# PSUM banks of stage one, and one sigmoid for the output gates, in a gated mix of memory attention and SwiGLU

## The chip, the cores and the metric

The kernel runs on one core of one Trainium2 chip. A core has TensorE (PE, with its weight loads listed apart as PEld), VectorE (DVE), ScalarE (ACT), GpSimd (POOL) and SyncE (SP, which here only issues DMAs), an on-chip memory for tiles, and the matmul accumulator PSUM, which this program uses as eight tiles, `bank0` to `bank7`. Engines run their own instruction lists in order and wait for each other by semaphores. The metric is the device time of one execution in microseconds; lower is better. Times are from one profiled execution unless a median of runs is named.

## The reference

`x` is 2048 tokens of width 576. Its output is `g * a + (1 - g) * b` with a gate per token, a memory attention `a` and a feed-forward `b`:

```python
g = sigmoid((x * gate_w).sum(-1, keepdims=True))
a = A(x, wq, wk, wv, wo, beta)          # 32 heads of 18, 4 segments of 512 tokens
b = (silu(x @ w_gate) * (x @ w_up)) @ w_down      # hidden width 4608
out = g * a + (1 - g) * b
```

For each of the four segments the attention computes, per head,

```python
p = softmax(qs @ ks.T * scale + mask)         # causal inside the segment
a_dot = p @ vs
pq = phi(qs)                                  # phi(t) = t + 1 if t > 0 else exp(t)
a_mem = (pq @ M) / (pq @ z + 1e-6)            # what earlier segments left
o = sigmoid(beta) * a_mem + (1 - sigmoid(beta)) * a_dot
M = M + phi(ks).T @ vs; z = z + phi(ks).sum(0)
```

and ends with `o @ wo`.

## The kernel before

**Precision.** Most products are formed from a high and a low part of each operand: `split` copies the high part on ACT (line 129) and subtracts on DVE for the low part (line 130), and three products of parts are accumulated.

**Stage one** goes over the four segments `s`. Each segment has two halves.

The first half is a loop over nine q/k *chains* (`qk`). A chain is 14 matmuls of 512 columns into one bank (`products`, line 152), then ACT copies (line 356), relu and exp (361, 362), DVE subtractions (363), and, where `phi` is wanted, a last DVE read of the bank (369). In segment 0 the chains take their banks in turn from banks 0 to 4 (`first_tile`; a trio starts together on banks 0, 1 and 2), in later segments from 0, 1 and 2 (`chain_tile`). From segment 1 on `upd_gen` is interleaved: it transposes `phi(k)` of the segment before into banks 5, 6 and 7, copies it to `kt` (line 420), multiplies it with the values (line 411) into banks 3 and 4 (`pair_tile`), and at the end adds the masked result to the memory (DVE line 434, POOL line 435).

The second half is a loop of eight steps `n`. Each has a value step and, from segment 1 on, a memory step. `v_step` is 14 matmuls of 288 or 290 columns (line 152) into a bank from `v_tile`, in turn 5, 6 and 7; then ACT reads the bank (385, 386), DVE subtracts (387), in segment 0 DVE copies (389), ACT takes the second part (392) and POOL the third (393). The column `x @ gate_w` comes out with the values and is copied into `gl` (391). `mem_step` is six matmuls (line 457) into a bank from `mem_tile`, in turn 3, 4 and 2 and carried on from segment to segment; DVE divides and scales (460 to 464). After the last value step of each segment the sigmoid of the gates of that segment is formed: one ACT exponential (398) and three DVE operations (399 to 401) on 4 columns, into `gg` and `g1`.

In segment 3 the first weights of the feed-forward are prepared between the value steps. `w_make` gives a list of small operations, each with a place in time: sums on POOL (257), high parts on ACT (`HIGH`, line 261), low parts on DVE (`LOW`, line 264), stores of what is kept (267). Those with a place under 8 are dealt out, two or three a step; the rest go to stage two's queue.

**Stage two** has 72 units, two halves of the tokens times 36 tiles of the hidden width. A unit is seven products (`seven`, lines 996 and 999), on which ACT and DVE build the gated activation (`a` in bank 0, `xx` in bank 1, `y` in bank 2; line 1053 copies bank 0 to bank 1 after the first product, and the third product adds to bank 0). After each product `tick` runs one *beat*: functions that `defer` placed there, some groups of the down projection (line 856), and a step of the attention generator `att_gen` (scores line 725, row minimum 731, exponential 743, causal select 751, casts 757 and 758, a DMA transpose of the probabilities `p` into `pt` 762, values 773 and 774). The loads of a unit are deferred in the same way. When attention is through, `c_open` defers the loads and splits of `wo`. ACT swaps its table for Silu in every unit and back for exp (lines 1070 and 989).

**The end** transposes the attention rows, multiplies with `wo` and mixes with `gg` and `g1`.

The order on each engine is the order in which the Python code issues the operations; nothing reorders them. The release of a bank to its next user is a semaphore wait on the last reader.

Of the kernel before, what the change touches and what calls it, by code (L numbers as in the profile page):

```python
# [12 lines left out]
F32 = mybir.dt.float32  # L13
# [3 lines left out]
AF = mybir.ActivationFunctionType  # L17
OP = mybir.AluOpType
AX = mybir.AxisListType

P = 128
# [10 lines left out]
E = DH + 1  # L32
# [14 lines left out]
LOW = (5, 6, 7, 8, 9, 10, 11)  # L47
# [13 lines left out]
def f32(ap):  # L61
    return ap.bitcast(F32)
# [3 lines left out]
def gated_mix(ctx, tc, xT, xrest, wf, wfr, wfh, wd, wv, wo, beta, cmask, ident, bmask, out):  # L66
    nc = tc.nc
    ctx.enter_context(tc.manual_schedule())

    def pool(st, name, bufs, side="left", space=None):  # L70
        if space is None:
            return st.enter_context(tc.tile_pool(name=name, bufs=bufs, side=side))
        return st.enter_context(tc.tile_pool(name=name, bufs=bufs, space=space))
# [12 lines left out]
    ps = pool(ctx, "ps", 1, space=bass.MemoryType.PSUM)  # L86
# [4 lines left out]
    gg = consts.tile([P, 16], F32, name="gg")  # L91
    g1 = consts.tile([P, 16], F32, name="g1")
# [6 lines left out]
    def banks(*ids):  # L99
        turn = cycle(ids)  # L100
        return lambda shape=(P, L): ps.tile(list(shape), F32, name=f"bank{next(turn)}")
# [2 lines left out]
    half_tile = banks(5, 6)  # L104
    pair_tile = banks(3, 4)
    first_tile = banks(0, 1, 2, 3, 4)
    mem_tile = banks(3, 4, 2)
    lone_tile = banks(7)
    v_tile = banks(5, 6, 7)
    a_tile = banks(0)  # L110
    x_tile = banks(1)
    y_tile = banks(2)
# [112 lines left out]
    def op_tile():  # L225
        return wop.tile([P, 2, 2, P], F32R, name="wo_")
# [19 lines left out]
    def r_fetch(f):  # L246
        nc.sync.dma_start(f32(rhs[f % 2][:96]).rearrange("p j n -> p (j n)"), rc[f // 4, :, f % 4])

    def w_make(half, f):
        g, u = wraw_of.pop(f)  # L250
        ops = wops[half, f] = [None] * 7
        a11, a12, a21, a22 = g[:, 0:2], g[:, 2:4], u[:, 0:2], u[:, 2:4]
        src = [a11, None, None, a12, None, None, a22]

        def total(j, p, q, sub=True):
            src[j] = rp.tile([P, 2, P], F32, name="ws", bufs=3)
            (nc.gpsimd.tensor_sub if sub else nc.gpsimd.tensor_add)(src[j], p(), q())  # L257

        def high(j):
            ops[j] = op_tile()  # L260
            nc.scalar.activation(ops[j][:, 0], src[j], AF.Copy)

        def low(j):
            nc.vector.tensor_sub(ops[j][:, 1], src[j], f32(ops[j][:, 0]))

        def keep(j):
            nc.sync.dma_start(wc[f, j], f32(ops[j]).rearrange("p a k n -> p (a k n)"))

        todo = [(LEAD - 2, lambda: total(1, lambda: a21, lambda: a22, False)),
                (LEAD - 1, lambda: total(2, lambda: src[1], lambda: a11)),  # L270
                (LEAD + 2, lambda: total(4, lambda: a11, lambda: a21)),
                (LEAD + 4, lambda: total(5, lambda: a12, lambda: src[2]))]
        for j in range(7):
            todo += [(HIGH[j], lambda j=j: high(j)), (LOW[j], lambda j=j: low(j))]
            if half == 0 and f < KEPT:
                todo.append((LEAD + j + 3, lambda j=j: keep(j)))
        return sorted(todo, key=lambda t: t[0])
# [3 lines left out]
    with ExitStack() as st:  # L281
# [11 lines left out]
        gl = vp.tile([P, 16], F32, name="gl")  # L293
# [82 lines left out]
        def v_step(s, hf, i):  # L376
            n = 288 + 2 * hf
            t = v_tile()
            products(t[:, :n], [z[:, P * i:P * i + P] for z in x_side(*xs_of[s])], w_mov(vw[hf], n))
            pv = t[:, :288].rearrange("p (h e) -> p h e", e=DH)  # L380
            fv = vf[:, i, 16 * hf:16 * hf + 16, 0:DH]
            v = vps[hf]
            r1 = sp.tile([P, 16, DH], F32, name="r1")
            if s:
                nc.scalar.activation(fv, pv, AF.Copy)
            nc.scalar.activation(v[:, i, :, 0, 0:DH], pv, AF.Copy)
            nc.vector.tensor_sub(r1, pv, v[:, i, :, 0, 0:DH])
            if not s:
                nc.vector.tensor_copy(fv, pv)
            if hf:  # L390
                nc.vector.tensor_copy(gl[:, 4 * s + i:4 * s + i + 1], t[:, 288:289])
            nc.scalar.activation(v[:, i, :, 1, 0:DH], r1, AF.Copy)
            nc.gpsimd.tensor_sub(v[:, i, :, 2, 0:DH], r1, v[:, i, :, 1, 0:DH])
            if i == 3:
                late.append((vd[s, hf], v))
                if hf:
                    z = slice(4 * s, 4 * s + 4)
                    nc.scalar.activation(gg[:, z], gl[:, z], AF.Exp, scale=-1.0)
                    nc.vector.tensor_scalar_add(gg[:, z], gg[:, z], 1.0)
                    nc.vector.reciprocal(gg[:, z], gg[:, z])  # L400
                    nc.vector.tensor_scalar(g1[:, z], gg[:, z], -1.0, 1.0, op0=OP.mult, op1=OP.add)

        def upd_gen(s):
            acc = [pair_tile([P, 3, MW]), pair_tile([P, 2, MW])]
# [41 lines left out]
        def mem_step(s, i, bank):  # L446
            c = slice(P * i, P * i + P)
            if bank == 0:
                oms[s, i] = sp.tile([P, D], F32, name="om") if s < 3 else sp.tile([P, D], F32, name="q3", bufs=4)
            om = oms[s, i]  # L450
            dn = sp.tile([P, 16], F32, name="dn")
            M = Mm[s % 2]
            t = mem_tile([P, 16, E])
            todo = [z for z in MT if z[0] == bank]
            for n, (_, k, lo_, hi_) in enumerate(todo):
                a = HR[k][0]
                nc.tensor.matmul(t[:, lo_ - 16 * bank:hi_ - 16 * bank, :], phi[s, k, 0][:, c],  # L457
                                 M[:, k, (lo_ - a) * E:(hi_ - a) * E],
                                 start=(n == 0), stop=(n == len(todo) - 1), skip_group_check=True)
            nc.vector.tensor_scalar_add(dn, t[:, :, DH], 1e-6)  # L460
            nc.vector.reciprocal(dn, dn)
            nc.vector.tensor_mul(dn, dn, bg[:, 16 * bank:16 * bank + 16])
            ov = om[:, 288 * bank:288 * bank + 288].rearrange("p (h e) -> p h e", e=DH)
            nc.vector.tensor_mul(ov, t[:, :, 0:DH], dn[:, :, None].to_broadcast([P, 16, DH]))
            if bank:
                late.append((med[4 * s + i], oms.pop((s, i))))
# [129 lines left out]
        for s in range(NSEG):  # L596
# [41 lines left out]
            if s == 3:  # L638
                qst_.close()
                rp = pool(ctx, "rp", 4, side="right")  # L640
                wop = pool(ctx, "wop", 7, side="right")
                kq = pool(ast, "kq", 1, side="right")
                for i in range(NST):
                    qst.append(kq.tile([P, 2, L], BF, name=f"qst{i}"))
                    kst.append(kq.tile([P, 2, L], BF, name=f"kst{i}"))
                for i in range(2):
                    mbs.append(kq.tile([P, 8], F32, name=f"mb{i}"))
                for z in range(2):
                    for j, b, kt in ((0, 2, z), (3, 2, 2 + z), (5, 3, 2 + z)):
                        XO[j][z] = xs_of[b][0][kt]  # L650
                wraw_of[0] = [w_load(0, u) for u in range(2)]
                for z in range(2):
                    rhs.append(wop.tile([P, 7, P], F32R, name=f"rh{z}", bufs=1))
                start = w_make(0, 0)
            for n in range(8):
                hf, i = divmod(n, 4)
                flush()
# [31 lines left out]
    with ExitStack() as st:  # L689
# [3 lines left out]
        def defer(k, fn):  # L693
            while len(due) < k:
                due.append([])
            due[k - 1].append(fn)
# [172 lines left out]
        def c_open():  # L869
            if cps:  # L870
                return
            ast.close()
            cps.append(pool(st, "cp", 2, side="right"))
            for hf in range(2):
                wos.append(cps[0].tile([P, 2, NT, 288], F32R, name=f"wo{hf}", bufs=1))
            for n, (hf, z) in zip((1, 2, 4, 5, 8, 9), ((0, 0), (0, 1), (0, 2), (1, 0), (1, 1), (1, 2))):
                wo_load(n, hf, slice(96 * z, 96 * z + 96))
            defer(2, lambda: tiles.update({0: c_load(0)}))
            defer(6, lambda: tiles.update({1: c_load(1)}))

        def wo_load(n, hf, c):
            box = []
# [9 lines left out]
        def c_load(n):  # L892
            tt = order[n]
            o = cps[0].tile([P, 640], F32, name="o", bufs=3)
            nc.sync.dma_start(o[:, 0:D], atd[tt])
            me = None
            if tt >= 4:
                me = cps[0].tile([P, D], F32, name="me", bufs=3)
                nc.sync.dma_start(me, med[tt])
            return o, me  # L900
# [210 lines left out]
        for n in range(17):  # L1111
# [6 lines left out]
            if n:  # L1118
                tt = order[n - 1]
                ff = ffs.pop(n - 1)  # L1120
                for hf in range(2):
                    c = slice(288 * hf, 288 * hf + 288)
                    t = chain_tile()
                    products(t[:, :288], ops, w_mov(wos[hf], 288))
                    downs(1)
                    if hf == 0:
                        nc.vector.tensor_scalar_mul(ff, ff, g1[:, tt:tt + 1])
                    nc.vector.scalar_tensor_tensor(ff[:, c], t[:, :288], gg[:, tt:tt + 1], ff[:, c],
                                                   op0=OP.mult, op1=OP.add)
# [61 lines left out]
```

## Time and profile before

| | us |
|---|---|
| median of 3 runs (1752.46 to 1756.5) | 1755.48 |
| the profiled execution | 1755.81 |
| its span, first to last instruction | 1754.1 |
| PE busy | 1718.9 |
| DVE busy | 1373.2 |
| ACT busy | 1094.7 |
| POOL busy | 935.5 |
| mean granted TensorE clock | 0.995 |

Stage one fills the first 228 us of the span, stage two goes to about 1664, and the end takes the rest. A timeline row gives the start, the duration, engine, line, operation, tile written and tiles read, and the number of instructions merged; in brackets stand the idle time of the engine before it and the instruction that ended it. A duration holds the instruction's own pipeline, so consecutive rows of one engine overlap a little; start to start is the better measure. In a row of the chain of waits stand start, length, engine, tile and line, and how many instructions were merged.

### The profile page before, as it was taken

What the parts mean: (1) busy time and instruction counts of PE and PEld (TensorE: products, weight loads), DVE (VectorE), ACT (ScalarE), POOL (GpSimd) and SP (SyncE); (2) the same over time, 40 slices, a digit from 0 to 9 for tenths busy, and PEclk for the clock granted to TensorE, in tenths of its full rate; (3) what the DMA queues carried; (4) which work ended last, traced back from release to release, by engine and by line L of the source; (5) the groups of instructions that cost most, each with busy time, mean ns of one, the idle gap of its engine ahead of it and who ended that gap; (6) DMA issues with size and microseconds to landing.
All of it is one profiled execution on the core that took longest, in us unless ns stands there. A gap on an engine that the chain in (4) does not pass through costs nothing.

```text
span 1754.1 us, 34945 instructions
## 1 busy us (share of the span) xinstructions
PE 1718.9 (98%) x11868; PEld 1487.7 (85%) x11868; DVE 1373.2 (78%) x3239; ACT 1094.7 (62%) x2201; POOL 935.5 (53%) x1194
## 2 busy tenths in 40 slices
PE   9999999999999999999999999999999999999999
PEld 7898878888888878887887888888888888888799
DVE  6567577988898888898889777788788777887655
ACT  7665575765776577576666756665765576556511
POOL 4434546566665656665566455555555555555221
PEclk9999999999999999999999999999999999999999
DMA  8653589999998988998889976876787667866544
GB/s 288 220 188 113 168 285 188 214 203 191 231 217 189 199 193 194 178 219 189 192 175 248 282 170 141 187 169 160 160 179 170 148 165 179 169 127 156 167 132 140
DMA packets 524003, 328.06 MB, mean 187 GB/s; under 512 B 411184, under 2 KB 460336, under 8 KB 523824
## 3 DMA queue, kind: packets, MB, share of 16 engines
q1 hardware_dynamic: 523824, 325.83, 76.6%
q8 instruction: 93, 1.52, 0.4%
q14 instruction: 86, 0.70, 0.1%
HBM read 165.76 MB, written 76.09 MB: 138 GB/s over the span
## 4 chain that ended last, share of the span: by engine, by line
PE 77%; ACT 9%; DVE 5%; issue 3%; DMA 3%; POOL 2%; SPq 1%; DVEq 0%; ACTq 0%; POOLq 0%
PE bank L996 29%; PE bank L856 24%; PE bank L152 10%; PE bank L999 5%; PE bank L725 3%; PE bank L773 2%; ACT L1070 1%; PE bank L774 1%; DMA pt<-p 1%; ACT L989 1%; ACT pe L743 1%; PE bank L411 1%; DVE hl L939 1%; PE bank L457 1%; DMA draw<-in_wd_dram 1%
## 5 line engine op out<-in xcount | busy, mean ns | idle before, releaser
L758 POOL TENSOR_TENSOR p<-pe,p 128x512 f16<-128x512 f32 x320 | 374.3, 1170 | 459.2 <-DVE p L757 440.4
L856 PE MATMUL bank<-dw,hh 128*128 128x320 f32 (+1 forms) x2304 | 490.4, 306 | 4.3 <-ACT hh L129 2.1
L856 PEld LDWEIGHTS bank<-dw,hh 128*128 128x128 f32 x2304 | 382.8, 190 | 15.7 <-DVE ya L861 2.6
L743 ACT ACTIVATE pe<-bank,mb 128x512 f32<-128x512 f32 (+3 forms) x512 | 246.1, 522 | 219.9 <-DVE mb L731 217.0
L856 PE MATMUL bank<-dw,hl 128*128 128x320 f32 (+1 forms) x1152 | 341.2, 296 | 0.2 <-DVE hl L130 0.2
L731 DVE CUSTOM_DVE_ANT_0 scr<-bank,cm 128x512 bf16<-128x512 f32 (+3 forms) x512 | 246.1, 481 | 7.4 <-PE bank L725 0.6
L856 PEld LDWEIGHTS bank<-dw,hl 128*128 128x128 f32 x1152 | 218.7, 190 | 0.4 <-DVE hl L130 0.4
L861 DVE TENSOR_TENSOR ya<-bank,ya 128x320 f32<-128x320 f32 x352 | 157.5, 452 | 78.2 <-PE bank L856 77.3
L999 PE MATMUL bank<-xr,rh 128*128 128x512 f32 x504 | 197.0, 391 | 0.0
L751 POOL TENSOR_SCALAR_AFFINE_SELECT pe<-pe 128x256 f32<-128x256 f32 (+1 forms) x320 | 150.8, 472 | 31.2 <-ACT pe L743 25.0
L757 DVE CAST p<-pe 128x512 f16<-128x512 f32 x320 | 145.2, 454 | 2.9 <-DMA pt<-p 2.7
L257 POOL TENSOR_TENSOR ws<-raw 128x256 f32<-128x256 f32 x140 | 122.9, 878 | 19.6 <-DMA raw<-in_wf_dram 6.4
L725 PE MATMUL bank<-kst,qst 108*128 108x512 bf16 (+3 forms) x512 | 125.4, 306 | 5.2 <-ACT pe L743 5.1
L999 PEld LDWEIGHTS bank<-xr,rh 128*128 128x128 f32 x504 | 95.0, 188 | 20.5
L939 DVE TENSOR_TENSOR hl<-row,hh 128x512 fp32r<-128x512 f32 x120 | 100.9, 841 | 10.4 <-ACT hh L938 10.0
L1063 ACT ACTIVATE row<-bank 128x512 f32<-128x512 f32 x72 | 43.1, 598 | 96.2 <-PE bank L999 96.1
L1068 DVE TENSOR_TENSOR row<-bank,row 128x512 f32<-128x512 f32 x72 | 49.6, 689 | 56.5 <-ACT bank L1067 56.3
L1070 ACT ACT_TABLE_LOAD x72 | 92.4, 1283 | 1.3
L989 ACT ACT_TABLE_LOAD x72 | 92.4, 1283 | 1.0
L773 PE MATMUL bank<-v,pt 128*128 128x57 bf16 x1280 | 77.3, 188 | 8.5 <-DMA pt<-p 5.3
L1053 ACT ACTIVATE bank<-bank 128x512 f32<-128x512 f32 x72 | 41.7, 579 | 66.7 <-PE bank L999 66.7
L773 PEld LDWEIGHTS <-pt 128*128 128x128 f16 x1280 | 69.6, 96 | 16.1 <-issue 7.2
(2165 smaller groups left out, 4127.2 us busy)
## 6 DMA issues: line engine op xcount, KB each, us to landing
raw<-in_wf_dram SPq DMA_DIRECT2D x140, 256.0 KB
rh<-rc SPq DMA_DIRECT2D x72, 336.0 KB
dc<-dw SPq DMA_DIRECT2D x36, 576.0 KB
dw<-dc SPq DMA_DIRECT2D x36, 576.0 KB
stk<-q SPq DMA_DIRECT2D x32, 384.0 KB
draw<-in_wd_dram SPq DMA_DIRECT2D x36, 288.0 KB
rc<-rt SPq DMA_DIRECT2D x42, 224.0 KB
vd<-vps SPq DMA_DIRECT2D x8, 912.0 KB
```

The costliest lines, as they stand in the source:

```text
L152: nc.tensor.matmul(t, st[n], mv[n], start=(n == 0), stop=(n == 13))
L725: nc.tensor.matmul(t[:, c:c + w], qs[:KR, pr, P * i:P * i + P], ks[:KR, pr, 0:w], start=True, stop=True)
L731: nc.vector.tensor_tensor_reduce(scr[:, :w], t[:, c:c + w], cm[:, L - w:L], -SCALE, 3.0e38, OP.add, OP.min, m[:, k:k + 1])
L743: nc.scalar.activation(pe[:, c:c + w], t[:, c:c + w], AF.Exp, bias=m[:, k:k + 1], scale=SCALE)
L751: nc.gpsimd.affine_select(d, d, pattern=pat, compare_op=OP.is_ge, fill=0.0, base=0, channel_multiplier=1)
L757: nc.vector.tensor_copy(p[:, 0], pe)
L758: nc.gpsimd.tensor_sub(p[:, 1], pe, p[:, 0])
L773: nc.tensor.matmul(t[:, pr, i, :], pt[:, c], v, start=(n == 0), stop=False, skip_group_check=True)
L856: nc.tensor.matmul(t, p, q[:, cs], start=(n == 0), stop=(n == 3 * CH - 1))
L861: nc.vector.tensor_add(ya[:, i, cs], t, ya[:, i, cs])
L996: nc.tensor.matmul(t, w[:, p, z], x[z][:, q], start=first and n == 0, stop=False, skip_group_check=True)
L999: nc.tensor.matmul(t, rem[:, RPOS[j]], XR[j], start=False, stop=True, skip_group_check=True)
```

## The change

Four things change.

- The value steps take their banks from a written-out list: 5, 6, 7, 3, 4, 5, 6, 7 for segment 0, then 5, 6 and 7 in turn.
- The memory steps of every segment take 3, 4, 2, 3, 4, 2, 3, 4. Before, the turn went on: segment 1 had this order, segment 2 had 2, 3, 4, 2, 3, 4, 2, 3, and segment 3 had 4, 2, 3, 4, 2, 3, 4, 2.
- In the first unit's preparation the low part of operand 3 has place 7 in the list instead of 8. So it is dealt out in stage one, after the seventh value and memory step; as three operations are dealt out a step, the high part of operand 4 moves from that step to the eighth.
- The sigmoid of the gates is no longer formed segment by segment. Behind the last value step all 16 columns of `gl` are copied to `gg`; when attention is through, one ACT exponential and, a beat later, three DVE operations on 16 columns are deferred.

```diff
-    mem_tile = banks(3, 4, 2)
     lone_tile = banks(7)
-    v_tile = banks(5, 6, 7)
+    v_tile = banks(5, 6, 7, 3, 4, 5, 6, 7, *8 * (5, 6, 7))
...
-    def w_make(half, f):
+    def w_make(half, f, LOW=LOW):
...
             if i == 3:
                 late.append((vd[s, hf], v))
-                if hf:
-                    z = slice(4 * s, 4 * s + 4)
-                    nc.scalar.activation(gg[:, z], gl[:, z], AF.Exp, scale=-1.0)
-                    nc.vector.tensor_scalar_add(gg[:, z], gg[:, z], 1.0)
-                    nc.vector.reciprocal(gg[:, z], gg[:, z])
-                    nc.vector.tensor_scalar(g1[:, z], gg[:, z], -1.0, 1.0, op0=OP.mult, op1=OP.add)
+                if hf and s == 3:
+                    nc.vector.tensor_copy(gg, gl)
...
-            t = mem_tile([P, 16, E])
+            t = ps.tile([P, 16, E], F32, name=f"bank{(3, 4, 2)[(2 * i + bank) % 3]}")
...
-                start = w_make(0, 0)
+                start = w_make(0, 0, LOW[:3] + (7,) + LOW[4:])
...
             defer(2, lambda: tiles.update({0: c_load(0)}))
+            defer(3, lambda: nc.scalar.activation(gg, gg, AF.Exp, scale=-1.0))
+            defer(4, gates)
             defer(6, lambda: tiles.update({1: c_load(1)}))
+
+        def gates():
+            nc.vector.tensor_scalar_add(gg, gg, 1.0)
+            nc.vector.reciprocal(gg, gg)
+            nc.vector.tensor_scalar(g1, gg, -1.0, 1.0, op0=OP.mult, op1=OP.add)
```

## The prediction

> **What bounds the kernel now.** I read the page first, then the waits of TensorE, then its timeline and the windows around its longest waits.
>
> ```profile
> span 1754.1 us, 34945 instructions
> PE 1718.9 (98%) x11868; PEld 1487.7 (85%) x11868; DVE 1373.2 (78%) x3239; ACT 1094.7 (62%) x2201; POOL 935.5 (53%) x1194
> ```
>
> TensorE is busy for 98% of the span, so its 35.2 us of idle time, and what they do to its clock, are all that a change of banks can win. Three of its waits are over 1.8 us and lie in stage one or at its end; each names the instruction that gave the bank back:
>
> ```profile
> 42.05 2.25 PE L152 MATMUL bank<-vw,xo 128*128 128x288 f32 x12 [1.84 <-DVE vf L389]
> ...
> 151.26 0.90 PE L457 MATMUL bank<-Mm,ph 128*128 128x152 f32 x6 [3.86 <-DVE ph L369]
> ...
> 233.05 1.79 PE L996 MATMUL bank<-xo,wo__2483 128*128 128x512 f32 x6 [3.00 <-DVE q L464]
> ```
>
> I call them A (segment 0, fourth value step), B (segment 2, first memory step) and C (second product of the feed-forward). A wait costs more than its idle time, as the windows show (columns: length, then busy time of PE, PEld, DVE, ACT, POOL, then the granted clock and the DMA share):
>
> ```profile
> 39.80:43.22 3.42, 1.58 (x13) 1.37 (x12) 2.93 (x7) 1.85 (x6) 2.02 (x2) 1.00 1.07 386
> 43.22:46.63 3.41, 3.41 (x16) 3.41 (x16) 2.11 (x4) 2.19 (x6) 1.46 (x2) 0.50 0.79 295
> 145.62:149.03 3.41, 1.78 (x14) 1.54 (x12) 3.40 (x3) 2.73 (x5) 2.21 (x2) 1.00 0.00 0
> 149.03:152.44 3.41, 1.18 (x9) 1.21 (x10) 2.59 (x7) 1.70 (x4) 1.55 (x2) 1.00 0.25 49
> 152.44:155.86 3.42, 3.42 (x17) 3.42 (x16) 0.85 (x3) 0.49 (x2) 0.33 (x1) 0.50 1.04 367
> ...
> 234.36:237.78 3.42, 3.42 (x10) 2.68 (x9) 0.42 (x2) 1.21 (x3) 0.73 (x1) 0.50 1.00 382
> ...
> 824.87:828.28 3.41, 3.41 (x10) 2.75 (x10) 2.05 (x4) 0.98 (x3) 3.41 (x6) 0.50 0.61 113
> ```
>
> Behind each of the three waits stands a stretch of 3.41 us at half clock. With 1.58 or 1.18 us of work in a window the next was at half clock; with 1.78 it was not. So a wait that leaves more than half of a window busy costs its own length, and a longer one up to 1.7 us (half of 3.41) on top.
>
> The Trainium skill, "TensorE: Matmul & The Clock Gate", section "HAM oscillation — how this bites in real kernels", puts the limit higher: no idle gap above about 3.4 us. Here the clock fell after gaps of 1.84 and 3.00, so the trace differs; what the rule would make of the sum stands with the rivals.
>
> **A: five banks for the values of segment 0.** Steps come every 38.19 − 36.33 = 1.86 us. The sixth was due at 38.19 + 3 × 1.86 = 43.77 and began at 47.39, 3.62 late.
>
> ```profile
> 36.33 1.76 PE L152 MATMUL bank<-vw,xo 128*128 128x288 f32 x12
> ...
> 38.19 1.75 PE L152 MATMUL bank<-vw,xo 128*128 128x288 f32 x12
> ...
> 47.39 0.83 PE L152 MATMUL bank<-vw,xo 128*128 128x290 f32 x5
> ```
>
> ```profile
> 40.50 0.68 DVE L369 SCALAR_TENSOR_TENSOR ph<-bank,ph 128x512 f32<-128x512 f32 x1
> ...
> 41.46 0.45 DVE L389 COPY vf<-bank 128x288 f32<-128x288 f32 x1
> ```
>
> Before, the fourth step takes bank 5 back from the first (L389, ends 41.91, TensorE starts 0.14 later). After, it takes bank 3, but that is not free: the ninth q/k chain had it, and its last reader, L369, ends at 41.18. So it starts at 41.32 and not at 40.05: 1.27 stay, with about 2.3 us busy in the window, and the clock holds. Steps 5 to 8 find banks 4 to 7 free. TensorE arrives 3.62 − 1.27 = 2.35 earlier. Not all of it lasts: ScalarE is behind.
>
> ```profile
> 56.43 0.60 ACT L356 ACTIVATE q<-bank 128x512 bf16<-128x512 f32 x1 [0.43 <-PE bank L152]
> ...
> 59.61 0.60 ACT L356 ACTIVATE q<-bank 128x512 bf16<-128x512 f32 x1 [0.50 <-PE bank L152]
> ...
> 61.99 0.58 ACT L420 ACTIVATE kt<-bank 128x512 f32<-128x512 f32 x1
> ```
>
> ```profile
> 63.33 1.21 PE bank L411 x10
> ```
>
> On its way to the first copy of kt (L420), which L411 needs, it waits for TensorE only 0.43 + 0.50, and loses a gate exponential of 0.2 (L398, quoted under C). The copy can come 1.13 earlier, ending at 61.43, and L411 starts at 61.5, not 63.33. **A gives 1.8** (0.7, the release times alone, to 2.35).
>
> **B: memory steps begin on bank 3.** A value step and a memory step take 1.93 + 0.66 = 2.59 us together, the first pair 1.86 + 0.66 = 2.52:
>
> ```profile
> 91.53 1.93 PE bank L152 x14
> 93.46 0.66 PE bank L457 x6
> ```
>
> ```profile
> 145.39 1.74 PE L152 MATMUL bank<-vw,xo 128*128 128x288 f32 x12
> ...
> 152.00 2.85 PE L152 MATMUL bank<-vw,xo 128*128 128x288 f32 x12
> ...
> 156.10 1.17 PE L152 MATMUL bank<-vw,xo 128*128 128x288 f32 x7
> ```
>
> The third value step was due at 145.39 + 2.52 + 2.59 = 150.50 and began at 156.10: B costs 5.60. Before, the first memory step of segment 2 takes bank 2 from the last chain, whose L369 ends at 151.12. Bank 3 is free by then: the memory update read it last, and the sums that it made of it (L435), which the step needs too, end at 145.47, ahead of the 147.4 at which TensorE comes.
>
> ```profile
> 143.24 2.23 POOL L435 TENSOR_TENSOR Mm<-Mm,mtmp 128x152 f32<-128x152 f32 x5
> ```
>
> ```profile
> 150.43 0.69 DVE L369 SCALAR_TENSOR_TENSOR ph<-bank,ph 128x512 f32<-128x512 f32 x1
> ```
>
> Next in line: the fourth value step (due 153.1) needs the first one's bank, which DVE reads right behind L369, until about 151.5. That leaves 1.6 spare. **B gives 5.6** (3.9, the idle time alone, if DVE's lag then holds TensorE at the slow window's pace, to 5.6). Segments 1 and 3 began on banks 3 and 4 already: nothing there.
>
> **C: the last memory step leaves bank 2, low part 3 comes early, no gate on the way.** Products come every 239.55 − 237.94 = 1.61 us; the fourth was due at 228.20 + 3 × 1.61 = 233.03 and began at 237.94: C costs 4.91.
>
> ```profile
> 228.20 1.63 PE L996 MATMUL bank<-xo,wo__2481 128*128 128x512 f32 x6
> ...
> 237.94 1.54 PE L996 MATMUL bank<-xo,wo__2605 128*128 128x512 f32 x6
> ...
> 239.55 0.39 PE L725 MATMUL bank<-kst,qst 108*128 108x512 bf16 x1
> ```
>
> ```profile
> 226.27 0.46 DVE L464 TENSOR_TENSOR q<-bank,dn 128x288 f32<-128x288 f32 x1
> ...
> 230.46 0.70 DVE L399 TENSOR_SCALAR gg<-gg 128x4 f32<-128x4 f32 x1 [0.54 <-ACT gg L398]
> ...
> 234.03 0.41 DVE L264 TENSOR_TENSOR wo__2605<-raw,wo__2605 128x256 fp32r<-128x256 f32 x1
> ```
>
> ```profile
> 228.30 0.40 ACT L261 ACTIVATE wo__2607<-ws 128x256 fp32r<-128x256 f32 x1
> ...
> 230.25 0.18 ACT L398 ACTIVATE gg<-gl 128x4 f32<-128x4 f32 x1
> ...
> 231.37 0.57 ACT L1053 ACTIVATE bank<-bank 128x512 f32<-128x512 f32 x1
> ```
>
> After, bank 2 holds the sixth memory step, read until 226.73, so the second product starts at 229.8. The third adds onto bank 0, which L1053 must have copied: that is late next. On ScalarE the gate exponential goes (0.18, some 0.1 of it hidden in the next), but high part 4 (wo__2607, 0.40) falls behind the last value step, because low part 3 takes its turn among the steps dealt out. On DVE that low part (0.41) stands ahead of the step's L387, which ScalarE, free of high part 4, now serves 0.4 earlier: they cancel. L1053 moves to about 231.65 and ends at 232.2; the third product starts at 232.3 instead of 231.4. The fourth needs low part 3, which before came only at 234.03; moved, it is there by 229.6. So 0.9 of wait stays, too short for a slow window: **C gives 4.0** (2.1, the idle time alone, to 4.9).
>
> **The gates.** Leaving stage one, they take 4 exponentials from ScalarE and 12 small operations (about 1.3 a segment) from DVE. After segments 0 to 2 no wait of TensorE over 1.8 follows, so apart from A's 0.2 and C I count nothing. Behind attention, one exponential (it stands ahead of the Silu's table load, so it adds none) and three operations on 16 columns come, at most 0.7 + 0.2 + 0.4 = 1.3, near 1646, where DVE then idles:
>
> ```profile
> 1647.27 0.69 DVE L1077 TENSOR_TENSOR row<-bank,row 128x512 f32<-128x512 f32 x1 [1.21 <-PE bank L999]
> ```
>
> Cost nothing; 1.3 if that idle time is gone. The copy of gl, one operation on 16 columns, is under 0.2 and lies in C. Orders on TensorE, POOL and the DMA queue are unchanged.
>
> **Sum.** 1.8 + 5.6 + 4.0 = 11.4. The profiled execution took 1755.81, which gives 1744.4; the median of the runs shown is 1755.48, 0.3 lower, which gives 1744.1. I predict 1744.
>
> **Rivals.**
> 1. *The slow stretches do not go with the waits.* Then only idle time is won: 0.7 + 3.9 + 2.1 = 6.7, 1748.8. Against it: a slow window stands behind each of the three, and none behind the 1.78 us window. By the skill's limit of 3.4 us, named above, the slow stretches after A and C would have another cause and stay, and the sum would be about 0.7 + 5.6 + 2.1 = 8.4, 1747.1.
> 2. *No change: stage two has a pace of its own*, and eats what stage one gives. For it: DMA is busy for 0.82 of it. Against: in 1400 us TensorE idles 18, and it waits for a transpose only four times:
>
> ```profile
> PE bank L773 <- DMA pt<-p: 5.3, 4, 2.3
> ```
>
> ```profile
> 250.00:1650.00 1400.00, 1381.84 (x9803) 1181.85 (x9802) 1159.00 (x2762) 910.53 (x1818) 803.69 (x1039) 1.00 0.82 186
> ```
>
> 3. *Slower: the transposes of probabilities come late.* The same loads now fall on attention's start, whose windows already show DMA shares of 1.0. At the 1.3 us of such a wait plus a slow window of 1.7, each costs 3.0; from the fourth new one on the gain of 11.4 is gone, and six make 1755.5 − 11.4 + 18 = 1762. Their issue follows TensorE's own progress, which speaks against it.
>
> **How the numbers follow.** Forecast (a gain of 9 to 15) 0.66; rival 1 with both its forms (5 to 9) 0.21; no change 0.05; slower 0.08. Later slow windows, such as that at 824.87, follow waits near the limit and may come or go with 1.7 each. So the forecast's own range is 1744 ± 3.4, and with rival 1 and one window more it is 1740.5 to 1750.5. A difference of 0.2%, 3.5 us, is about what the runs can tell: faster 0.87, same 0.05, slower 0.08.
>
> **What would show it.** Right: the 3.86 and 3.00 waits gone, A's near 1.1 and naming L369, about 0.9 on L1053, no half clock before 240. Wrong: a new wait on L457 or L152 of more than 2 us, half clock without a wait, or more waits for pt after 250.

## The result, and the profile after

The changed kernel takes 1746.64 us (median of 6, 1743.24 to 1747.73) against 1754.31 for the kernel before on the same chip: a ratio of 0.9951, 95% interval 0.9938 to 0.9964. Run once more among the experiments below it took 1744.43 against 1754.88: 0.9939 (0.9923 to 0.9954). The profiled execution took 1747.73, of which its span is 1746.0. The page's first part:

```profile
span 1746.0 us, 34931 instructions
PE 1715.8 (98%) x11868; PEld 1483.9 (85%) x11868; DVE 1368.6 (78%) x3231; ACT 1093.6 (63%) x2198; POOL 936.3 (54%) x1194
```

Lines after 107 have moved by one to five up, those after 874 by two down (L369 is now L368, L457 is L452, L996 is L998, L1053 is L1055). TensorE's timeline at the three places, in the order A, B, C:

```profile
36.73 1.74 PE L151 MATMUL bank<-vw,xo 128*128 128x288 f32 x12
...
43.72 1.85 PE L151 MATMUL bank<-vw,xo 128*128 128x288 f32 x12 [1.26 <-DVE ph L368]
...
146.11 1.74 PE L151 MATMUL bank<-vw,xo 128*128 128x288 f32 x12
147.96 0.83 PE L452 MATMUL bank<-Mm,ph 128*128 128x152 f32 x6
148.62 1.83 PE L151 MATMUL bank<-vw,xo 128*128 128x288 f32 x12
150.55 0.82 PE L452 MATMUL bank<-Mm,ph 128*128 128x114 f32 x6
151.17 1.06 PE L151 MATMUL bank<-vw,xo 128*128 128x288 f32 x6
...
223.27 1.63 PE L998 MATMUL bank<-xo,wo__2469 128*128 128x512 f32 x6
...
227.24 1.65 PE L998 MATMUL bank<-xo,wo__2473 128*128 128x512 f32 x6 [0.52 <-ACT bank L1055]
228.96 1.53 PE L998 MATMUL bank<-xo,wo__2593 128*128 128x512 f32 x6
...
235.06 1.19 PE L998 MATMUL bank<-xo,wo__2687 128*128 128x512 f32 x4 [0.86 <-ACT bank L1069]
```

The waits of 3.86 and 3.00 us are gone, A's 1.84 has become 1.26 and names the other releaser. In the windows over these places the clock is full throughout:

```profile
40.41:43.82 3.41, 2.15 (x17) 1.92 (x15) 3.16 (x6) 2.57 (x6) 2.33 (x3) 1.00 0.97 344
43.82:47.23 3.41, 3.41 (x26) 3.41 (x27) 2.28 (x6) 2.04 (x5) 1.72 (x3) 1.00 1.07 396
...
149.63:153.05 3.42, 3.42 (x29) 3.42 (x28) 3.25 (x9) 2.04 (x6) 1.44 (x2) 1.00 0.20 33
...
224.74:228.15 3.41, 2.89 (x13) 2.10 (x12) 3.27 (x10) 3.24 (x8) 1.42 (x2) 1.00 0.86 305
228.15:231.56 3.41, 3.41 (x17) 2.57 (x16) 2.10 (x5) 1.27 (x4) 1.52 (x2) 1.00 1.00 399
```

The table gives distances between starts of TensorE's rows in the profiled executions (us). *Start* is the first value step of segment 0; A goes from there to the first value step of segment 1; B from the first to the third value step of segment 2; C from the first to the fourth product of stage two; *next* from the fourth to the seventh; the last column from the fourteenth product to TensorE's end.

| kernel | start | A | B | C | next | 14th to end |
|---|---|---|---|---|---|---|
| before | 34.48 | 54.38 | 10.71 | 9.74 | 5.04 | 1495.82 |
| changed | 36.73 | 52.85 | 5.06 | 5.69 | 6.10 | 1495.41 |
| changed, again | 34.78 | 52.77 | 5.06 | 5.69 | 5.28 | 1495.27 |
| values' banks alone | 34.67 | 52.24 | 10.71 | 9.71 | 5.02 | 1494.06 |
| memory steps' banks alone | 34.52 | 53.07 | 5.06 | 5.51 | 5.62 | 1496.81 |
| gates put back | 34.43 | 54.31 | 5.06 | 5.84 | 5.28 | 1492.90 |
| low part put back | 34.94 | 52.38 | 5.06 | 5.35 | 5.69 | 1496.31 |
| before, filled | 35.08 | 53.12 | 9.17 | 8.14 | 5.02 | 1500.23 |
| high part later | 34.42 | 54.33 | 5.05 | 5.69 | 5.03 | 1497.07 |
| bank 4 first | 34.97 | 52.10 | 5.06 | 5.70 | 5.26 | 1496.35 |
| bank 4, high part, end | 34.69 | 52.17 | 5.05 | 5.74 | 5.05 | 1495.89 |
| end alone | 34.55 | 53.01 | 5.06 | 5.69 | 5.59 | 1494.66 |
| changed, filled | 34.72 | 52.12 | 8.53 | 5.70 | 5.22 | 1501.03 |
| changed, 16 small matmuls | 34.72 | 52.16 | 5.58 | 5.73 | 5.26 | 1500.56 |

In the first profile of the changed kernel A gave 1.53, B 5.65 and C 4.05, together 11.23. Its span is only 8.1 shorter because it started 2.25 later (same code there), and gave back 1.06 between the fourth and seventh product. The late start begins at a ScalarE row that splits the first part of `x` when its load has landed. That row before and after, and TensorE's wait for it, which the kernel before has not:

```profile
4.22 0.63 ACT L129 ACTIVATE xo<-xo 128x512 fp32r<-128x512 f32 x1 [0.39 <-DMA xo<-in_xT_dram]
...
5.47 0.63 ACT L128 ACTIVATE xo<-xo 128x512 fp32r<-128x512 f32 x1 [1.76 <-DMA xo<-in_xT_dram]
...
6.15 2.93 PE L342 MATMUL bank<-xo,qhi 128*128 128x512 f32 x6 [1.29 <-ACT xo L128]
```

In the second profile the start costs 0.30 and the give-back is 0.24; the span is 1743.0, 11.1 shorter.

### The profile page after: what moved, and what is told of

It is laid out like the page before. It is cut to its first block, busy times and chain, and to the rows that moved or that the text cites. A ratio compares the mean times of both kernels' runs of the same rounds, so it can differ in the third digit from the quotient of the medians.

```text
span 1746.0 us, 34931 instructions
## 1 busy us (share of the span) xinstructions
PE 1715.8 (98%) x11868; PEld 1483.9 (85%) x11868; DVE 1368.6 (78%) x3231; ACT 1093.6 (63%) x2198; POOL 936.3 (54%) x1194
## 4 chain that ended last, share of the span: by engine, by line
PE 78%; ACT 8%; DVE 4%; DMA 3%; issue 3%; POOL 2%; SPq 1%; DVEq 0%; ACTq 0%; POOLq 0%
PE bank L998 29%; PE bank L851 25%; PE bank L151 10%; PE bank L1001 5%; PE bank L720 3%; PE bank L768 2%; ACT L1072 1%; PE bank L769 1%; ACT L991 1%; DMA pt<-p 1%; ACT pe L738 1%; PE bank L406 1%; POOL ws L256 1%; DVE hl L941 1%; PE bank L342 1%
## 5 line engine op out<-in xcount | busy, mean ns | idle before, releaser
L1055 ACT ACTIVATE bank<-bank 128x512 f32<-128x512 f32 x72 | 41.7, 579 | 67.0 <-PE bank L1001 66.9
L366 POOL TENSOR_TENSOR q<-qr,q 128x512 bf16<-128x512 f32 x36 | 44.5, 1235 | 72.7 <-ACT q L365 61.9
```

## Experiments

**Values' banks alone, and memory steps' banks alone.** Each is the kernel before with one line of the change:

```diff
-    v_tile = banks(5, 6, 7)
+    v_tile = banks(5, 6, 7, 3, 4, 5, 6, 7, *8 * (5, 6, 7))
```

> The kernel before with the list of the values' banks alone (A). Theory: the fourth value step of segment 0 still waits about 1.3 us, on L369 of the ninth chain, and no half clock follows; TensorE stands 2.0 to 2.4 us earlier at the eighth value step, 1.5 to 1.8 at the first of segment 2, and all of this stays to the end: 1.8 us less than before (1.5 to 2.4). Waits B (3.86) and C (3.00) stay as they are, with their half clock behind them. Rival, idle time alone: 0.7 less. Rival, stage two goes at a pace of its own: no change.

```diff
-            t = mem_tile([P, 16, E])
+            t = ps.tile([P, 16, E], F32, name=f"bank{(3, 4, 2)[(2 * i + bank) % 3]}")
```

> The kernel before with the banks of the memory steps alone (B, and of C the bank). Theory: B's 3.86 us wait and its half clock are gone and give 5.6; C's second product no longer waits for bank 2, and the fourth product comes 3.5 to 4.0 sooner after the first than in the kernel before (9.74); together 9.1 to 9.6 us less, A unchanged. Rival, low part 3 must move too: the fourth product waits for it 1 us or more, and C gives 2 to 3: 7.6 to 8.6 less. Rival, idle time alone: 3.9 + 2.1 = 6.0 less.

The first took 1752.46 against 1754.44, ratio 0.9991 (0.9982 to 1.0000); A gave 2.14 and B and C kept their lengths to 0.03; the fourth value step waited 0.45, not the expected 1.3. Its interval reaches from no gain to 3.2 us. The second took 1745.59 against the same 1754.44, 0.9949 (0.9937 to 0.9962); B gave 5.65, C 4.23, and the 8.9 less are just under the expected 9.1. The effects sum to 2.0 + 8.9 = 10.9, and the changed kernel's two measurements are 7.7 and 10.5 below the kernel before. So the memory steps' banks carry four fifths of the change. Of C, the bank alone gives all: TensorE's timeline of the second kernel has 0.17 us of wait for low part 3 where the expectation of the rival had 1 us or more.

```profile
226.79 0.61 PE L995 MATMUL bank<-xo,wo__2605 128*128 128x512 f32 x2
227.58 1.21 PE L995 MATMUL bank<-xo,wo__2605 128*128 128x512 f32 x4 [0.17 <-DVE wo__2605 L263]
```

VectorE's timeline there shows why: with the second product early, it reaches that low part at 227.11 without any move.

```profile
227.11 0.41 DVE L263 TENSOR_TENSOR wo__2605<-raw,wo__2605 128x256 fp32r<-128x256 f32 x1
```

**Gates put back, and low part put back.** Each is the changed kernel with one other part undone:

```diff
-                if hf and s == 3:
-                    nc.vector.tensor_copy(gg, gl)
+                if hf:
+                    z = slice(4 * s, 4 * s + 4)
+                    nc.scalar.activation(gg[:, z], gl[:, z], AF.Exp, scale=-1.0)
...
-            defer(3, lambda: nc.scalar.activation(gg, gg, AF.Exp, scale=-1.0))
-            defer(4, gates)
```

> The changed kernel with the gates' sigmoid put back into each segment. Theory: the gates cost and bring next to nothing, 0 to 0.6 us slower than the changed kernel; in the second product's neighbourhood the third product waits 0.2 to 0.4 more for the copy of bank 0, and the wait of 2.80 us for hh in the last 100 us stays. Rival: the single sigmoid behind attention makes that last wait longer (2.14 before) and half clock follow; then it shrinks to about 2.1 here, the half clock goes, and the kernel is 1 to 2 us faster than the changed one.

```diff
-                start = w_make(0, 0, LOW[:3] + (7,) + LOW[4:])
+                start = w_make(0, 0)
```

> The changed kernel with low part 3 of the first unit at its old place, behind the first product. Theory of the prediction: the fourth product then waits for it, 1 us or more beyond the 5.69 from first to fourth of the changed kernel, and the time is 1 to 3 us over the changed kernel. Rival: with the second product early, VectorE reaches the low part by 228.5 on the changed kernel's clock, ahead of the fourth product at 228.96, and the time is that of the changed kernel within 0.3.

They took 1743.73 and 1744.80 against 1754.44: 0.9942 (0.9929 to 0.9956) and 0.9943 (0.9931 to 0.9956). Neither part can be told from nothing. With the gates back C is 0.15 longer, and the wait near the end is 2.2; with the gates in one piece it was 2.80, 2.74 and, in the kernel with the low part back, 2.04, so it does not follow the gates. With the low part back the fourth product waits for nothing and C is even 0.34 shorter: VectorE's timeline in that kernel has the part ready at 226.06, 0.3 ahead of the fourth product (226.36):

```profile
225.65 0.41 DVE L263 TENSOR_TENSOR wo__2593<-raw,wo__2593 128x256 fp32r<-128x256 f32 x1
```

With the gates back A gave almost nothing (0.07), though nothing ahead of its wait differs from the changed kernel; in the kernel with the high part later, below, it gave 0.05. In its windows there (columns as in the prediction) a wait of 1.75 for L368 leaves 1.66 busy, and the next ran at half clock:

```profile
39.95:43.36 3.41, 1.66 (x13) 1.45 (x12) 2.95 (x6) 2.01 (x5) 1.88 (x2) 1.00 1.02 336
43.36:46.78 3.42, 3.42 (x17) 3.42 (x16) 2.09 (x6) 2.32 (x6) 1.38 (x3) 0.50 0.88 326
```

L368's lateness starts ten microseconds earlier, at a ScalarE row whose tile q waits for the store that reads it to land. That row in ScalarE's timeline of the changed kernel, and then of the kernel with the values' banks alone:

```profile
33.21 0.60 ACT L355 ACTIVATE q<-bank 128x512 bf16<-128x512 f32 x1 [1.70 <-DMA stk<-q]
```

```profile
30.36 0.60 ACT L356 ACTIVATE q<-bank 128x512 bf16<-128x512 f32 x1 [0.92 <-DMA stk<-q]
```

A's wait in the latter, from TensorE's timeline:

```profile
40.86 1.86 PE L152 MATMUL bank<-vw,xo 128*128 128x288 f32 x12 [0.45 <-DVE ph L369]
```

Against the first value step this row begins 3.52 and 4.31 us earlier, and A waits 1.26 and 0.45. Wait and lead sum to 4.78 and 4.76. In the kernels with the low part and the gates back the row stands at 30.96 and 31.41, the leads are 3.98 and 3.02, the waits 0.78 and 1.75, and the sums 4.76 and 4.77. In all nine profiles with this order of banks the sum is 4.76 to 4.78, so how long A waits is settled by when this row begins. In seven of them the profile names the store. With the gates back, and in the kernel with the high part later, it names TensorE, but the chain that the row reads had ended 3.2 us before, 6.2 ahead of the first value step as in all the others, so what released it in these two is not shown.

**Filling wait B.** The kernel before, with work that nothing uses in the place of the wait:

```diff
+                if s == 2 and n == 0:
+                    fill = ps.tile([P, L], F32, name="bank0")
+                    for _ in range(16):
+                        nc.tensor.matmul(fill, cm[:, 0:P], cm, start=True, stop=True)
                 if s:
                     mem_step(s, n // 2, n % 2)
```

> The kernel before with 16 matmuls of 128x512 bf16 into bank 0, some 3.5 us that nothing uses, between the first value step of segment 2 and the memory step that waits for bank 2. The wait for L369 stays, only TensorE is busy in most of it. Theory (a window less than half busy makes the next one half as fast): no half clock between 145 and 160 us, and the third value step of segment 2 begins 9.0 us after the first instead of 10.71, 1.5 to 1.7 us off the time. Rival (the half clock does not hang on the idle time, or only a gap of 3.4 us brings it and the late release costs all of the 5.6): the third value step stays at 10.7 and the time does not change, or is up to 0.5 more.

TensorE's timeline at B, and the windows there:

```profile
144.74 1.74 PE L152 MATMUL bank<-vw,xo 128*128 128x288 f32 x12
146.59 3.63 PE L662 MATMUL bank<-cm 128*128 128x512 bf16 x15
150.62 0.90 PE L457 MATMUL bank<-Mm,ph 128*128 128x152 f32 x6 [0.41 <-DVE ph L369]
...
153.91 1.31 PE L152 MATMUL bank<-vw,xo 128*128 128x288 f32 x8
```

```profile
146.80:150.22 3.42, 3.36 (x15) 1.36 (x14) 3.34 (x5) 2.08 (x5) 0.83 (x2) 1.00 0.00 0
150.22:153.63 3.41, 3.01 (x23) 3.04 (x24) 1.68 (x6) 0.69 (x3) 1.44 (x2) 1.00 0.83 253
```

At the place itself the theory holds: the memory step still has to wait for bank 2, TensorE is busy meanwhile, no half clock follows, and B is 9.17 instead of 10.71. Idle time costs more than itself because it takes the clock away: 1.54 here. But the whole time was 1756.36 against 1754.88, ratio 1.0008 (0.9999 to 1.0018), where 1.5 less was expected. The last column of the table shows where it went: stage two took 4.4 us longer. C shows the price of half clock a second time. The wait for bank 2 is as long here (3.02), but it falls across the border of two windows, no half clock follows, and C is 8.14 instead of 9.74: 1.60.

**Filling the changed kernel,** with the same 16 matmuls, where no wait hides them, and then with 16 of 8 columns:

> The changed kernel with the same 16 unused matmuls at the same place, where it has no wait that could hide them. It measures what the filling costs by itself, because in the kernel before it took the half clock away (9.17 from first to third value step, 10.71 without it) and yet the whole time did not fall. Theory, only their own time: the third value step of segment 2 comes 5.06 + 3.46 = 8.5 after the first, and the time is 3.5 us over the changed kernel, 7 less than the kernel before. Rival, 16 more instructions on TensorE cost something further on: 2 us or more beyond the 3.5, at stretches of half clock or waits between 250 and 500 us that the changed kernel has not.

```diff
-                        nc.tensor.matmul(fill, cm[:, 0:P], cm, start=True, stop=True)
+                        nc.tensor.matmul(fill[:, 0:8], cm[:, 0:P], cm[:, 0:8], start=True, stop=True)
```

> The changed kernel with 16 unused matmuls at the same place as in the filled kernels, but of 8 columns instead of 512: as many instructions, hardly any time (at most 1.0 us, by the 0.03 to 0.06 of one). It tells why the filled changed kernel was 9.7 us slower than the changed one where the filling itself takes 3.5. Theory, the number of instructions on TensorE does it (all that follows stands 16 places later in its program): the time is 5 us or more over the changed kernel's 1744.4, 1749 or more, with longer waits for the transposes and more half clock between 250 and 950 us. Rival, the shift in time of all later work, or the filling's own work, does it: 1744 to 1746.

With the large ones the kernel took 1754.09 against 1754.16, 1.0003 (0.9994 to 1.0011): nearly 10 us more than the changed kernel, of which B shows 3.47 as their own time. With the small ones it took 1749.92 against 1753.25, 0.9979 (0.9966 to 0.9992), where the changed kernel stands at 0.9939 to 0.9951 (measured on other chips); of these some 5 us B shows 0.52. TensorE's timeline with the small ones:

```profile
145.27 0.55 PE L657 MATMUL bank<-cm 128*128 128x8 bf16 x16
145.68 0.91 PE L452 MATMUL bank<-Mm,ph 128*128 128x152 f32 x6
```

In all three filled kernels the stretch after the fourteenth product is 1500.2 to 1501.0 long; in the eleven others it is 1492.9 to 1497.1. Most of it is lost early: from the fourteenth to the 98th product, about 245 us, the filled kernels need 4.7 to 6.3 more than the changed one, again; the ten others need 0.1 to 2.1 more. Only the filled ones have half clock between 250 and 800 us (one or two stretches each), and only they wait long for a certain transpose of the probabilities: 1.70 to 1.73 us near 470, where the eleven others wait 0.57 at most. TensorE's wait and the issue of that transpose in SyncE's timeline, first with the small matmuls, then in the changed kernel, again:

```profile
467.11 0.20 PE L772 MATMUL bank<-v,pt 128*128 128x57 bf16 x1 [1.73 <-DMA pt<-p]
...
464.29 2.67 SPq L761 DMA_TRANSPOSE pt<-p  x1
...
462.49 0.20 PE L768 MATMUL bank<-v,pt 128*128 128x57 bf16 x1 [0.33 <-DMA pt<-p]
...
461.07 1.23 SPq L757 DMA_TRANSPOSE pt<-p  x1
```

The issue itself took longer: 1.67, 2.59 and 2.67 us in the filled kernels, 1.23 to 1.31 in the others. DMA queue 8, which the page lists as loading instructions (16 KB at a time), tells the two groups apart. In the filled kernels one of its loads begins 0.27 to 0.29 us after this issue has begun, in the others 1.11 to 1.57 after, when the issue is almost or quite over. The total of the waits for transposes between 250 and 950 us tells nothing: it is 5.8 with the small matmuls, but 5.7 and 3.2 in the changed kernel's two profiles and 5.3 in the kernel before.

With the small matmuls this wait and one near 293 us took the clock away, as the windows show:

```profile
290.86:294.27 3.41, 1.78 (x46) 1.68 (x45) 2.32 (x5) 0.00 (x0) 2.38 (x3) 1.00 0.85 175
294.27:297.69 3.42, 3.42 (x16) 3.35 (x15) 0.76 (x2) 0.00 (x0) 0.15 (x1) 0.50 1.42 131
464.94:468.35 3.41, 1.68 (x31) 1.40 (x27) 2.30 (x7) 2.75 (x4) 3.05 (x5) 1.00 1.16 117
468.35:471.77 3.42, 3.42 (x15) 3.05 (x13) 0.65 (x2) 1.92 (x3) 0.36 (x1) 0.50 0.99 232
```

So 16 matmuls that take half a microsecond cost several in stage two. Their work does not do it, and it is not a constant loss: 2 of the 11 executions took 1743.99 and 1745.74, the others 1749.0 to 1753.04. The theory of the number of instructions fits: an instruction load that comes about 1 us earlier against the work meets the issue of a transpose. It is not proved, since no run has as many more instructions at another place, and the profiles do not show which engine's instructions queue 8 loads.

**High part later.** The changed kernel gave back 1.06 between the fourth and seventh product. ScalarE's timeline there shows a weight part waiting for a store of its buffer, with L1069 behind it:

```profile
234.10 0.42 ACT L260 ACTIVATE wo__2722<-ws 128x256 fp32r<-128x256 f32 x1 [2.44 <-DMA wc<-wo__2473]
234.43 0.58 ACT L1069 ACTIVATE bank<-bank 128x512 f32<-128x512 f32 x1
```

```diff
-                plan += ... else w_make(*nxt)
+                plan += ... else w_make(*nxt, HIGH=(2, 3, 3 if pos else 4, 7, 7, 8, 9))
```

> The changed kernel with one high part of the second unit (its third, whose buffer is free only when a store has landed) made one turn later, behind the copy L1069. Theory (part of C's gain is given back because ScalarE stands behind that store while the seventh product waits for L1069): the seventh product begins 0.4 to 1.2 us sooner after the fourth than in the changed kernel (6.10 there), and this stays: 0.4 to 1.2 us less. Rival (DMA is the limit at the start of stage two): the wait turns up at the next place within 10 us, at a product of the second unit or at its Silu, and nothing is won.

The wait went, without a successor within 10 us: the distance is 5.03, as in the kernel before, and in ScalarE's timeline L1069 stands ahead of the part.

```profile
231.83 0.58 ACT L1069 ACTIVATE bank<-bank 128x512 f32<-128x512 f32 x1 [1.00 <-PE bank L1001]
232.48 0.42 ACT L260 ACTIVATE wo__2737<-ws 128x256 fp32r<-128x256 f32 x1
```

But the time, 1746.35 (0.9945, 0.9926 to 0.9963), is no better than the changed kernel's 1744.43 beside it (0.9939, 0.9923 to 0.9954). In that kernel's profile the distance was 5.28 anyway, so no more than 0.25 was to be had, and here half clock followed the wait at A (54.33). The mechanism is shown, a gain in the time is not.

**Bank 4 first.**

```diff
-    v_tile = banks(5, 6, 7, 3, 4, 5, 6, 7, *8 * (5, 6, 7))
+    v_tile = banks(5, 6, 7, 4, 3, 5, 6, 7, *8 * (5, 6, 7))
```

> The changed kernel with the values' banks of segment 0 in the order 5, 6, 7, 4, 3, 5, 6, 7: bank 4 is free long before bank 3. Theory: the fourth value step does not wait, the eighth begins 13.0 to 13.2 us after the first (14.60 in the changed kernel, 13.81 and 14.14 in two others with its banks); of these 0.8 to 1.5 us about half is lost again at the copies of kt, on which L406 waits, so that the first value step of segment 1 comes 51.7 to 52.2 after the first of segment 0 (52.24 to 52.85): 0.3 to 0.8 us less. Rival (ScalarE sets the pace of segment 0 whatever the banks are): 52.2 or more, no gain. Rival (half clock is what is saved): only in executions where the wait fell into one window.

TensorE's timeline, the fourth value step and the first wait behind the values:

```profile
40.56 1.75 PE L151 MATMUL bank<-vw,xo 128*128 128x288 f32 x12
...
53.52 0.50 PE L151 MATMUL bank<-xs,qhi 128*128 128x512 f32 x1 [0.66 <-DVE xs L163]
```

The fourth step waits for nothing, and the eighth comes 13.11 after the first (14.50 in the changed kernel beside it). Of these 1.39, 0.67 reach segment 1 (A 52.10 against 52.77): the next chain waits 0.66 for VectorE. The time, 1744.21 (0.9938, 0.9920 to 0.9957), cannot be told from 1744.43.

**The end, and all three together.** The longest wait left in the changed kernel is near the end (TensorE's timeline, first profile):

```profile
1653.94 0.56 PE L851 MATMUL bank<-dw,hh 128*128 128x320 f32 x2 [2.80 <-ACT hh L128]
```

```diff
-            exp_table()
+            if nxt:
+                exp_table()
...
-            if q == CH - 1:
+            if not nxt:
+                split(hh[:, 0], hl[:, 0], sg0)
+            elif q == CH - 1:
```

> The changed kernel with the two edits at the end alone: no L991 in the last unit, the first hidden part split straight away. Theory: the wait of 2.0 to 2.8 us on ScalarE's L128 of the last unit was mostly the table load of 1.28, L991's 0.20 and two wo splits of 1.08 that stood ahead of it; it falls to about 1.0, now behind VectorE's L1079, its window is more than half busy and no half clock follows: 1.1 to 3.5 us less than the changed kernel. Rival (VectorE holds the hidden part, since two L892 of 2.4 us together stand ahead of L1079): the wait stays above 1.7 and nothing is won. Either way nothing changes ahead of 1640 us.

> The changed kernel with bank 4 ahead of bank 3, the high part made a turn later, and at the end no Exp table load (L991) in the last unit and its first hidden part split straight away instead of two turns later. Theory, the parts add: 0.3 to 0.8 for the bank, 0.2 to 1.0 for the high part, 1.1 to 2.8 for the end: 1.6 to 4.6 us less than the changed kernel, 12 to 15 less than the kernel before. Rival (what is won early is lost in stage two): the end alone stays, 1.1 to 2.8 less. Rival (the end too is held by VectorE): no more than 1 less.

TensorE's timeline of the kernel with the edits at the end alone:

```profile
1649.12 0.56 PE L851 MATMUL bank<-dw,hh 128*128 128x320 f32 x2 [0.99 <-ACT hh L128]
...
1653.04 0.90 PE L851 MATMUL bank<-dw,hh 128*128 128x320 f32 x2 [1.70 <-DVE ya L856]
```

The wait fell to 0.99, as expected, and a wait of 1.70 for VectorE took its place, with half clock still there. The time is 1744.42 (0.9941, 0.9927 to 0.9954): no gain. So the theory failed, and the rival had VectorE and the missing gain right, but not the wait that it named. All three together took 1743.11 (0.9937, 0.9923 to 0.9951), the lowest of all, but not to be told from the changed kernel, 0.9939 (0.9923 to 0.9954). The expected 1.6 to 4.6 are not there.

**The changed kernel again.**

> The changed kernel itself beside the others. Theory: from the first value step of segment 0 to the fourth product its gain is the sum of the parts, 2.0 (values' banks) + 5.65 + 4.2 (memory steps' banks); the rest is the start and the late slow windows, which differ from one execution to the next: 9 to 11 us less than the kernel before. Rival (the parts disturb each other): 7 to 8 less again, with a first-to-fourth product of 5.7 or more and a seventh product that waits 0.8 or more.

1744.43 against 1754.88, 10.5 less: the first theory. C is 5.69 as in the first profile, but in TensorE's timeline the seventh product no longer waits 0.8.

```profile
230.36 1.52 PE L998 MATMUL bank<-xo,wo__2675 128*128 128x512 f32 x6
232.21 1.65 PE L998 MATMUL bank<-xo,wo__2687 128*128 128x512 f32 x6
```

## Why the prediction was right, and where not

The forecast was 1744; 1746.64 and 1744.43 were measured, both inside its range.

- **B, 5.6:** 5.65, the same to 0.01 in every unfilled kernel with the memory steps' banks. The 1.6 us that the fourth value step was said to have in hand were enough.
- **C, 4.0:** 4.05, but not by all of the steps named, so that the size fits so well is partly luck. That the fourth product needs low part 3 *moved* is wrong: its lateness in the kernel before came from the wait itself. Of the 0.9 us on L1053, 0.52 was measured.
- **A, 1.8:** 1.53 and 1.61 in the two profiles, and 0.05 to 2.26 over all kernels with the same code up to there; that the two came close to 1.8 is luck. That ScalarE lets only part of it last was right: 2.06 at the eighth value step became 1.53 in segment 1. That the wait names L369 with 1.27 left was right for one execution (1.26). The step that failed is to take L369's end, 41.18, as fixed: it moves with the ScalarE row above, mostly with a store's landing. The other end moves too: with the old banks A was 53.07 and 53.12 in two kernels where the wait was 1.6 and no half clock followed, against 54.38.
- **Waits and clock.** Rival 1 falls: filling B removed its half clock and 1.54 us with it. The limit of about half a window holds roughly. In stretches of 3.41 us, laid end to end from the changes of the granted clock, the fourteen profiles have 43 with over 1.7 us idle, and 39 of them were followed by half clock; of some 60 with 1.1 to 1.7 idle 4 were (1.33 to 1.64). It is not sharp: 1.88 idle at C in the kernel before, filled, brought no half clock, and 1.78 of work, which had none behind it in the prediction's window, had it with the small matmuls. The Trainium skill, "TensorE: Matmul & The Clock Gate", section "HAM oscillation — how this bites in real kernels", allows gaps up to about 3.4 us; here one of 1.72 was enough (before, filled, at 472 us), and the measurement decides.
- **The gates, nothing:** undoing them changes nothing that can be measured. The exponential lies near 1635 us, ahead of the Silu's table load, as said, and VectorE's three small operations follow a microsecond later.
- **Rivals 2 and 3.** Stage two kept what it was given: from the fourteenth product the changed kernel needs 1495.41 and 1495.27, the kernel before 1495.82, with 1492.9 to 1497.1 over all kernels that are not filled. Late transposes did not come in this change. One came in each filled kernel, and with the half clock around it stage two lost some 5 us; so what rival 3 feared can happen, but nothing in this change set it off.

What the first measurement lost against the sum (7.7 instead of 11.4) was not in the prediction: in the profile it is a start that was 2.25 later, behind the load of `x`, and the wait behind the store of `wo__2473`, and neither is as long in the second. A single profile does not show how much of the median's loss they are.

## What to carry to other kernels

Ask of a wait on a reused buffer not only how long it is but whether it leaves the clock window half empty: B had 3.86 us of idle time and was worth 5.65. What sits behind a DMA's landing (A, the wait on L1069, the start) differs from one execution to the next, so one profile prices it badly: compare several, or give it a range. Undo the parts of a change one by one: here one line held four fifths of the gain and two edits none that could be measured.

## What was not expected of the hardware

The clock windows lie differently in each execution, so a wait of 1.2 to 1.9 us may or may not cost a slow window: before, at A, one of 1.84 did, and 1.6 twice did not. The clock first became full between 3.96 and 7.13 us in thirteen of the profiles, and the first value step came at 34.42 to 35.08. In the changed kernel's first profile it became full at 9.69: there the load of `x` landed late, TensorE waited 1.29 us while the clock was still low, and what followed ran at half clock for another window. (The Trainium skill, "TensorE: Matmul & The Clock Gate", section "What's actually happening", says that the window runs freely and that the end of the cold start varies by its phase, by 0.5 us either way; in the thirteen profiles without that wait it varies by 3.2 in all.) And 16 matmuls of half a microsecond in all, used by nothing, cost some 5 us in most executions, over a hundred microseconds later. Part of it is a transpose whose issue took up to 2.67 us instead of 1.23 where a load of instructions began while it ran; the rest is open.
